# Sliding-window units behind full units 6 to 29, a cap on product runs per slot, later reciprocals

## The chip, the cores and the metric

One Trainium2 chip, one core of it. The metric is the device time of one execution in microseconds (us). Before the change three runs gave 967.66, 967.76 and 965.90 us, median 967.66.

## What is computed

Two attention blocks that share nothing but the shape: S = 2048 positions, D = 512, H = 32 heads of 16. The first ("full") attends to every position, the second ("sliding") to the last 256. The two outputs stand side by side in the last dimension.

```python
qkv = (x @ wqkv).reshape(B, S, 3, H, 16)          # q, k, v: (B, H, S, 16)
scores = einsum("bhqd,bhkd->bhqk", q, k) * 16 ** -0.5
# second block only: keep 0 <= i - j < 256, elsewhere -1e9
o = einsum("bhqk,bhkd->bhqd", softmax(scores), v)
out = concatenate([o_A @ wo_A, o_B @ wo_B], axis=-1)
```

## The kernel before, in words

**Units and slots.** Queries come in four quarters (`p`) of 512, heads in eight groups (`g`) of four, so each block has 32 units. A full unit has 64 jobs: 16 key tiles of 128 times four heads, each a 128 x 512 block of scores with keys on the partitions. A sliding unit has 12 jobs of up to 512 columns, whose scores begin with masks that TensorE adds by an identity product (line 242 into `sps`). `slots` (a method of the kernel class) lines all jobs for ScalarE up, two to a slot: one slot is one score buffer `sps` (two of them, in PSUM) and one exponential (`exps`, L521) into `pT`. There are 866 slots. The order of units is fixed: full unit k, then those sliding units whose place is k. `B_AT, B_END` spread the 32 sliding units evenly behind full units 9 to 29.

**Part of the exponentials lies on VectorE.** `D_KTS` and `D_N` give up to six of the sixteen key tiles of a full unit to VectorE, which turns a score block into an integer whose bits are an approximate exponential (`y`, L533). GpSimd, or for some VectorE, adds two shifts to it (`z`, L548), and three weighted copies of v (`va`, `v0x`, `v1x`) combine y and both z. These jobs ride as a third score matmul in a slot, in a bank of `dps`. `D_N` holds the number of such key tiles for each of the 32 full units; they sum to 175.

**Values.** `values` (L604) multiplies exponentials with v, in runs of four matmuls, one for each head in its own column group, and accumulates in one PSUM bank `op`. The first column of v is one, so that each head's first row is the sum of its exponentials. When a unit is done, `epilogue` copies the bank (`osb`, L650), gathers the four sums (`den`, a DMA, one slot later), takes the reciprocal on VectorE (`invert`, L659), sends it to DRAM and reads it back spread over 32 rows each (`rb`, L667), and multiplies on GpSimd (`on`, L673). `LAGS` holds how many slots after the copy the reciprocal, the spread read and the multiplication may start. The result goes through DRAM into `oT`, from which the output projection reads.

**Projections in between.** Keys, values, queries and outputs are projected in pieces, woven between the slots: a task is four pieces (`pieces`), each a run of four matmuls (`quad`, L242); after slot 30 there is one PSUM bank (`ms`) for all of them. After the last piece VectorE evacuates the bank. A query task also computes a bound of its scores (`magnitude`, then `guard` with `nega`, L388) which takes the bank once more. The projected keys and queries pass through DRAM scratch rows (`dka`, `dkb`, `dq`) to reach their layout.

**What sets the order.** The whole program is written out by a loop over slots in `run`, engine by engine in that order. `plan` gives each task a slot from which it may run (`nb`), a due slot and the tasks that must be done before it (`after`). In `run`, `rate` is the largest of (pieces up to a due slot) / (slots until then), at most 4; it adds to `credit`, at most 4, and each piece costs 1. In a slot `s` the loop writes: the exponential of s, DMAs that are due, VectorE's queue (`vector`), values and pieces (`fill`), then the scores of slot s + 2, then possibly one more piece. `used` counts the runs of the slot, `room` is 3, in slots that precede masked scores 2. In a slot without any run, a dummy run on mask data (`unread`) keeps TensorE at work: into the free projection bank, or, if that is taken or was just released (`extra`), into the score buffer itself ahead of the scores. A task becomes eligible when its `after` is done; DMA landings count as done a fixed number of slots after their issue (`LANDED`).

The x tiles of the sliding block take the places of the first two x tiles of the full block, so they are loaded, by a transposing DMA (L226), only when the queries of that full quarter are projected.

Of the kernel before, what the change touches and what calls it, by code (L numbers as in the profile page):

```python
# [20 lines left out]
NG = H // GH  # L21
# [5 lines left out]
S = 2048  # L27
D = 512
NC = D // P
NPASS = S // 512  # L30
# [3 lines left out]
QRING = (2, 2)  # L34
KRING_B = 6
VRING_B = 10
B_AT, B_END = 9, 29
EARLY = (0, 30)
LANDED = dict(x=14, w=10, wo=10, oT=8)
LAGS = (5, 10, 15)  # L40
ONES_BITS = 1.0019378662109375

LOG2E = 1.4426950408889634
# [5 lines left out]
BIAS = math.log(MEAN) - 127.0 * math.log(2.0)  # L49
NEG = -30000.0  # L50
D_KTS = (1, 4, 6, 9, 11, 14)
D_N = (0, 4, *(5,) * (NG - 2), *(6,) * (NPASS * NG - NG - 2), 5, 4)
D_LEAD = 24


# [52 lines left out]
class _Kernel:  # L108
# [36 lines left out]
    def scratches(self):  # L145
        zero = self.tile([P, 512], BF16, "y0", Y_BUFS)
        one = self.tile([P, 512], BF16, "y0", Y_BUFS)
        self.nc.gpsimd.memset(zero[:].bitcast(FP32), 0.0)
        self.nc.gpsimd.memset(one[:].bitcast(FP32), ONES_BITS)
        self.rows = {name: [self.dram.tile([2 * P, n], BF16, name=f"{name}{k}")  # L150
                            for k in range(bufs)]
                     for name, n, bufs in (("dq", 512, 4), ("dka", S, 2), ("dkb", 512, 3),
                                           ("do", 512, 4))}
        for name, head in (("dka", one), ("dq", None), ("dkb", one)):
            for t in self.rows[name]:
                n = t.shape[1] // 512
                t = t[:].rearrange("(h r) (c f) -> h r c f", r=32, f=512)
                self.nc.sync.dma_start(t[:, VP:, :, :], zero[0:8 * (32 - VP), :].unsqueeze(
                    1).broadcast_to((8 * (32 - VP), n, 512)))
                if head is not None:  # L160
                    self.nc.sync.dma_start(t[:, 0, :, :], head[0:8, :].unsqueeze(
                        1).broadcast_to((8, n, 512)))
# [249 lines left out]
    def q_steps(self, i, p, pr, free):  # L412
        def finish(bank):
            qs = self.q_copy(bank, self.nc.vector.tensor_copy)
            rows = self.scratch("dq")
            rows_of.append(rows)
            self.guarded += 1
            self.after(1, lambda: self.nc.sync.dma_start(rows[:, 1:VP, :], qs[:]))
            self.nega(i, pr, p)

            def magnitude():
                mq = self.q_abs(bank, qs)
                self.guards.append((self.slot + 3, lambda: guard(mq, rows)))
            return magnitude

        def guard(mq, rows):
            bank, alone = self.q_guard(i, p, pr, mq), not self.early()
            if alone:
                self.open = bank
            else:  # L430
                self.full += 1

            def lift():
                gs = self.q_lift(bank)
                if alone:
                    self.open = None
                    self.freed = self.slot
                else:
                    self.full -= 1
                self.guarded -= 1  # L440
                self.after(1, lambda: self.nc.sync.dma_start(rows[:, 0, :], gs[:]))
                self.after(max(5, free - self.slot), load)
            self.dve.append((self.slot + 1, 0.69, lift))

        def load():
            self.nc.sync.dma_start(self.q_tile(i, p, pr)[:],
                                   rows_of[0].rearrange("(g j) r f -> (j r) g f", g=2))
        rows_of = []
        return self.pieces(lambda: self.q_ops(i, p, pr)[0], lambda: self.q_ops(i, p, pr)[1],
                           finish)  # L450

    def out_steps(self, i, p, last=False):
        steps = []
# [522 lines left out]
    def plan(self, slots, done):  # L976
# [3 lines left out]
        begin, end, vneed = {}, {}, {}  # L980
# [6 lines left out]
        tasks = []  # L987
# [20 lines left out]
        for i in range(2):  # L1008
            for p, pr in q_order:
                old = before(q_order, (p, pr), QRING[i])  # L1010
                task(("q", i, p, pr), begin[i, p, 2 * pr] - (20 if (i, p, pr) == (0, 0, 1) else 28),
                     self.q_steps(i, p, pr, old and end[i, old[0], 2 * old[1] + 1] + 3 or 0),
                     [("qb",), *(("kx", 0, pr, c) for c in range(NPASS))] if i == 0
                     else [("kx", 1, pr, p), ("w", 1, 0)],
                     old and (i, old[0], 2 * old[1] + 1), 12)
            for p in range(NPASS):
                e = end[i, p, NG - 1] + LAGS[2] + 20
                if (i, p) != self.order[-1][:2]:
                    steps = self.out_steps(i, p)
                    for n in range(4):  # L1020
                        task(("o", i, p, n), e - 8 + 4 * n, steps[n * NC:(n + 1) * NC],
                             [("oT", i, p), ("wo", i)])
                    self.woven.add((i, p))
        for n, after in ((1, [("k", 0, pr) for pr in range(NPAIR)]),
# [3 lines left out]
        for c in range(NPASS):  # L1028
# [8 lines left out]
            for t in range(4 * c, 4 * c + 4):  # L1037
                old = t - VRING_B
# [3 lines left out]
            for pr in range(NPAIR):  # L1042
                old = before(q_order, (c, pr), KRING_B)
# [38 lines left out]
    def run(self):  # L1082
        self.orow, self.done, self.woven = {}, set(), set()
        self.start()
        done = self.done
        done |= {("v", 0, t) for t in range(2)} | {("q", 0, 0, 0), ("wo", 0)}
        slots = self.slots()
        tasks = self.plan(slots, done)
        credit = 0.0
        for s in range(2):  # L1090
            self.pick(s, slots[s])
            self.scores(slots[s])
        self.values_first()
        for s, sl in enumerate(slots):
            self.slot = s
            self.exps(s, sl)
            due = [x for x in self.later if x[0] <= s]
            self.later = [x for x in self.later if x[0] > s]
            for _, f in due:
                f()  # L1100
            self.vector(s, sl)
            rate, total = 0.0, 0
            for t in tasks:
                if t["nb"] <= s:
                    total += len(t["steps"])
                    rate = max(rate, total / max(1, t["due"] - s))
            credit = min(credit + min(rate, 4.0), 4.0)
            ahead = slots[s + 2] if s + 2 < len(slots) else None
            masked = bool(ahead) and bool(ahead["jobs"][0].blocks)
            room = 2 if masked else 3  # L1110
            used = self.values(s, room - (credit >= 1.0))
            while credit >= 1.0 and used < room + 1 and self.fill(s, tasks, done, False):
                credit -= 1.0
                used += 1
            if used < room:
                used += self.values(s, room - used)
            extra = False
            if len(self.banks) < 3 and self.near is not None and s >= len(slots) - 8 + 2 * len(
                    self.banks):
                tag, bufs = ("dps", 2) if len(self.banks) < 2 else ("ms", 1)  # L1120
                self.banks.append(self.ps.tile([P, 512], FP32, name=tag, tag=tag, bufs=bufs)[:])
                self.most(len(self.banks) - 1)
            elif not used and not self.banks and not self.early():
                extra = self.open is not None or s < self.freed + 2
                if not extra:
                    self.unread(self.bank()[:])
            if ahead:
                self.pick(s + 2, ahead)
                self.scores(ahead, extra)
            if (self.guards or credit >= 1.0) and (  # L1130
                    not masked or used < room or credit >= 3.0):
                if self.fill(s, tasks, done, True):
                    credit -= 1.0
                    used += 1
                while self.early() and credit >= 1.0 and used < room + 1 and self.fill(
                        s, tasks, done, True):
                    credit -= 1.0
                    used += 1
        assert not tasks, [t["name"] for t in tasks]
        while self.unit < len(self.order) or self.dve or self.later:  # L1140
            self.slot += 1
            due = [x for x in self.later if x[0] <= self.slot]
            self.later = [x for x in self.later if x[0] > self.slot]
            for _, f in due:
                f()
            self.bucket = 9.0
            self.vector(self.slot, slots[-1])
            self.values(self.slot, 1)
# [57 lines left out]
```

## Time and profile before

| engine | busy us | what for the most part |
|---|---|---|
| PE (TensorE) | 862.0 | scores, masks, values, projections |
| ACT (ScalarE) | 897.0 | 866 exponentials, L521 |
| DVE (VectorE) | 724.9 | y (L533, 700 times), evacuations, part of z |
| POOL (GpSimd) | 672.5 | z (L548, 524 half tiles), `on` (L673, 63 times) |

The profiled execution spans 966.7 us. A group in the page is read as: line, engine, operation, tile written <- tiles read, shapes, count, then busy time, mean ns of one, idle time of the engine just before, and who ended most of it. In a timeline a row is start, duration, engine, line, operation and tiles, with the idle time before and its releaser in brackets. In the answer by windows the columns are the window, its length, busy time and instruction count of PE, PEld (weight loads), DVE, ACT and POOL, the granted TensorE clock as a share of full speed, the DMA share and GB/s. In the waits a row is the waiting engine and tile, who released it, total us, times, and the longest.

DMA work is light on average: 70.02 MB in all, and the SyncE queue's packets took 23.7% of sixteen engines' span.

### The profile page before, as it was taken

To read this page: it belongs to the slowest core of one execution; us is meant where nothing else is said; L and a number is where in the kernel's file an instruction comes from. 1 tells how busy PE (TensorE), PEld (TensorE's weight loads), DVE (VectorE), ACT (ScalarE), POOL (GpSimd) and SP (SyncE) were. 2 spreads that over 40 slices of the span, in tenths; PEclk is the share of its full clock that TensorE was granted. 3 is DMA by queue.
4 is the path that set the end of the run, shared out by engine and by line. 5 is a ranking of instruction groups with operands and counts; after the bars stand their busy time and mean duration, and the time that the engine had idled before them with its cause. 6 is when DMAs were issued, how large, how long until landed. Compare 5 with 4: busy or idle time off the path is not lost.

```text
span 966.7 us, 29831 instructions
## 1 busy us (share of the span) xinstructions
PE 862.0 (89%) x12386; PEld 325.6 (34%) x12390; DVE 724.9 (75%) x1195; ACT 897.0 (93%) x883; POOL 672.5 (70%) x694
## 2 busy tenths in 40 slices
PE   7988888888899999989898889988989899898887
PEld 3322222223243324333343333433333334333322
DVE  4587987988886858878778688686886877857742
ACT  4889999999989979999999999999999999999995
POOL 2016887888858875968858678687686874976860
PEclk8999998999999979999999999999999999999978
DMA  8032314111212252122221224122212222221111
GB/s 253 14 92 92 96 41 129 57 37 40 69 57 78 83 103 62 46 81 84 64 63 63 76 71 109 57 70 81 76 56 57 85 75 64 80 74 42 41 35 44
DMA packets 84039, 70.02 MB, mean 72 GB/s; under 512 B 31080, under 2 KB 75072, under 8 KB 83904
## 3 DMA queue, kind: packets, MB, share of 16 engines
q1 hardware_dynamic: 82560, 67.60, 23.7%
q8 instruction: 96, 1.57, 0.7%
q10 hardware_dynamic: 1344, 0.52, 0.2%
q14 instruction: 39, 0.32, 0.1%
HBM read 42.73 MB, written 22.76 MB: 68 GB/s over the span
## 4 chain that ended last, share of the span: by engine, by line
ACT 46%; PE 36%; issue 11%; DVE 3%; DMA 3%; POOL 1%; SPq 0%; ACTq 0%; DVEq 0%; POOLq 0%
ACT pT L521 46%; PE sps L501 10%; PE op L604 9%; PE ms L242 7%; PE sps L242 5%; PE dps L501 2%; PE dps L242 2%; DMA da<-amax 1%; DVE y L533 1%; DMA y<-in_A_wqkv_dram 1%; PE ms L388 1%; DMA den<-osb 0%; POOL z L548 0%; PE dps L247 0%; PE dps L802 0%
## 5 line engine op out<-in xcount | busy, mean ns | idle before, releaser
L521 ACT ACTIVATE pT<-sps,bias 128x1024 bf16<-128x1024 f32 (+2 forms) x866 | 886.1, 1115 | 47.8 <-PE dps L501 24.7
L548 POOL TENSOR_SCALAR z<-y 128x1024 int16<-128x1024 int16 x524 | 570.0, 1088 | 231.4 <-DVE y L533 140.3
L533 DVE TENSOR_SCALAR y<-dps 128x512 int16<-128x512 f32 x700 | 468.0, 683 | 126.6 <-PE dps L501 111.3
L501 PE MATMUL sps<-qTa,kTa 32*128 32x512 bf16 x1348 | 265.5, 390 | 38.0 <-ACT pT L521 31.3
L501 PE MATMUL dps<-qTa,kTa 32*128 32x512 bf16 x700 | 271.8, 388 | 3.6 <-DVE y L533 1.7
L501 PEld LDWEIGHTS <-kTa 32*128 32x128 bf16 x2048 | 100.0, 91 | 255.0 <-issue 249.9
L242 PE MATMUL sps<-mask,ident 128*32 128x256 bf16 (+2 forms) x3116 | 128.0, 262 | 47.0 <-ACT pT L521 45.2
L604 PE MATMUL op<-pT,va 128*32 128x512 bf16 x1348 | 139.2, 395 | 1.1 <-ACT pT L521 0.9
L242 PEld LDWEIGHTS <-ident 128*32 128x32 bf16 x3360 | 88.8, 95 | 118.4 <-issue 101.3
L673 POOL TENSOR_TENSOR on<-osb,rb 128x512 bf16<-128x512 f32 x63 | 83.4, 1323 | 25.3 <-DMA rb<-dn 20.5
L548 DVE TENSOR_SCALAR z<-y 128x2048 int16<-128x2048 int16 x88 | 80.3, 913 | 5.2 <-PE op L604 1.0
L604 PEld LDWEIGHTS <-va 128*32 128x32 bf16 x2048 | 49.8, 95 | 82.2 <-issue 75.4
L501 PE MATMUL sps<-qTb,kTb 32*128 32x384 bf16 (+2 forms) x704 | 72.4, 276 | 0.0
L604 PE MATMUL op<-z,v1x 128*32 128x512 bf16 x700 | 71.9, 391 | 0.0
L604 PE MATMUL op<-z,v0x 128*32 128x512 bf16 x700 | 70.6, 390 | 0.0
L604 PE MATMUL op<-y,va 128*32 128x512 bf16 x700 | 69.5, 391 | 0.0
L650 DVE COPY osb<-op 128x512 f32<-128x512 f32 x63 | 42.8, 679 | 0.1
L394 DVE TENSOR_SCALAR ob<-ms 8x512 bf16<-8x512 f32 x31 | 20.9, 675 | 23.4 <-PE ms L388 22.0
L604 PE MATMUL op<-pT,vb 128*32 128x384 bf16 (+2 forms) x704 | 38.1, 280 | 0.0
L457 DVE CAST ob<-ms 128x512 bf16<-128x512 f32 x28 | 19.2, 685 | 21.5 <-PE ms L242 21.5
L242 PE MATMUL ms<-xlo,wq 128*32 128x512 bf16 x368 | 31.8, 383 | 0.5 <-DVE ob L394 0.2
L501 PEld LDWEIGHTS <-kTb 32*128 32x128 bf16 x704 | 21.0, 92 | 31.2 <-issue 27.8
(132 smaller groups left out, 491.4 us busy)
## 6 DMA issues: line engine op xcount, KB each, us to landing
rb<-dn SPq DMA_DIRECT2D x63, 256.0 KB
do<-on SPq DMA_DIRECT2D x62, 128.0 KB
kTb<-dkb SPq DMA_DIRECT2D x16, 256.0 KB
qTb<-dq SPq DMA_DIRECT2D x16, 256.0 KB
dq<-qs SPq DMA_DIRECT2D x31, 128.0 KB
qTa<-dq SPq DMA_DIRECT2D x15, 256.0 KB
out_dram<-ob SPq DMA_DIRECT2D x29, 128.0 KB
kTa<-dka SPq DMA_DIRECT2D x3, 1024.0 KB
```

What stands on the lines that cost most here:

```text
L242: self.nc.tensor.matmul(out[m], lhsT=lhsT[:, m], rhs=rhs, tile_position=(0, 32 * j), skip_group_check=True, **kw)
L388: self.nc.tensor.matmul(b[0:32, :], lhsT=self.nega(i, pr, p)[:], rhs=mq[:], start=True, stop=True, tile_position=(0, 0), skip_group_check= ...
L394: self.nc.vector.tensor_scalar(out=gs[:], in0=b[0:8, :], scalar1=LIFT, scalar2=None, op0=ALU.add)
L457: self.nc.vector.tensor_copy(out=ob[:], in_=bank)
L501: nc.tensor.matmul(at[b][:, o:o + q1 - q0], lhsT=kT[r, gg, k0:k0 + P], rhs=qT[r, gg, q0:q1], start=not jb.blocks, stop=True, tile_position ...
L521: nc.scalar.activation(out=pT[:, b:e, :n], in_=src, func=ACT.Exp, scale=SCALE, bias=self.bias[:])
L533: nc.vector.tensor_scalar(out=y[:, jb.j, :].bitcast(I16), in0=at[b], scalar1=0.0, scalar2=BITS, op0=ALU.max, op1=ALU.mult)
L548: eng.tensor_scalar(out=z[:, j:j + step].bitcast(I16), in0=grp["y"][:, j:j + step].bitcast(I16), scalar1=SHIFTS[n], scalar2=1.0, op0=ALU.a ...
L604: self.nc.tensor.matmul(u["t"][32 * j:32 * j + 32, q0:q1], lhsT=v[:, h * VP:h * VP + 32], rhs=src, start=(j not in u["started"]), stop=Fal ...
L650: nc.vector.tensor_copy(out=osb[:], in_=op[:])
L673: nc.gpsimd.tensor_mul(out=on[:], in0=osb[:], in1=st["rb"][:])
```

## The change

It moves the sliding units to full units 6 to 29, gives full unit 7 a sixth key tile on VectorE (the sum of `D_N` becomes 176), projects the second quarter of the full block's queries sooner (earlier due slots, a longer lead, eight `dq` scratch buffers instead of four, since their rows wait longer in DRAM for their place), makes the reciprocal and what follows it two slots later, gives output projections later due slots, and limits a slot to `room` runs, with one more where a task is late or the scores ahead are masked. The dummy run into the score buffer is left out ahead of masked scores. `nega` is computed with the first piece of a query task instead of after its last. The purpose is to even out TensorE's work between the slots, and to keep waits for DMAs and for GpSimd away from the queues that feed ScalarE.

```diff
-B_AT, B_END = 9, 29
+B_AT, B_END = 6, 29
-LAGS = (5, 10, 15)
+LAGS = (7, 12, 17)
-D_N = (0, 4, *(5,) * (NG - 2), *(6,) * (NPASS * NG - NG - 2), 5, 4)
+D_N = (0, 4, *(5,) * 5, *(6,) * 23, 5, 4)
...
-                     for name, n, bufs in (("dq", 512, 4), ("dka", S, 2), ("dkb", 512, 3),
+                     for name, n, bufs in (("dq", 512, 8), ("dka", S, 2), ("dkb", 512, 3),
...
-            self.nega(i, pr, p)
...
+        steps = self.pieces(lambda: self.q_ops(i, p, pr)[0], lambda: self.q_ops(i, p, pr)[1],
+                            finish)
+
+        def first(step=steps[0]):
+            self.nega(i, pr, p)
+            step()
+        return [first, *steps[1:]]
...
-                task(("q", i, p, pr), begin[i, p, 2 * pr] - (20 if (i, p, pr) == (0, 0, 1) else 28),
+                due = begin[i, p, 2 * pr] - (20 if (i, p, pr) == (0, 0, 1) else 28)
+                if (i, p) == (0, 1):
+                    due = min(due, begin[1, 1, 0] - 90 + 6 * pr)
+                task(("q", i, p, pr), due,
...
-                     old and (i, old[0], 2 * old[1] + 1), 12)
+                     old and (i, old[0], 2 * old[1] + 1), 84 if (i, p) == (0, 1) else 12)
...
-                        task(("o", i, p, n), e - 8 + 4 * n, steps[n * NC:(n + 1) * NC],
+                        task(("o", i, p, n), min(e + 6, len(slots) - 20) + 4 * n, steps[n * NC:(n + 1) * NC],
...
-            rate, total = 0.0, 0
+            rate, total, late = 0.0, 0, False
             for t in tasks:
                 if t["nb"] <= s:
+                    late = late or t["due"] < s + 2
...
-            while credit >= 1.0 and used < room + 1 and self.fill(s, tasks, done, False):
+            while credit >= 1.0 and used < room + (late or masked) and self.fill(
+                    s, tasks, done, False):
...
-                extra = self.open is not None or s < self.freed + 2
-                if not extra:
+                extra = not masked and (self.open is not None or s < self.freed + 2)
+                if self.open is None and s > self.freed + 1:
                     self.unread(self.bank()[:])
...
             if (self.guards or credit >= 1.0) and (
-                    not masked or used < room or credit >= 3.0):
+                    late or used < room or credit >= 3.0):
```

Here `e` is the last slot of the unit's quarter, plus `LAGS[2]`, plus 20.

More of the change, by code (lines that the diff above doesn't have):

```diff
@@ L448, in q_steps @@
         rows_of = []
-        return self.pieces(lambda: self.q_ops(i, p, pr)[0], lambda: self.q_ops(i, p, pr)[1],
-                           finish)
+        steps = self.pieces(lambda: self.q_ops(i, p, pr)[0], lambda: self.q_ops(i, p, pr)[1],
[4 more added lines that the diff above has]
+        return [first, *steps[1:]]
     def out_steps(self, i, p, last=False):
```

## The prediction, made before the changed kernel was run

> **What bounds the kernel now.** I read the page's busy shares first, then the costliest groups, the waits, and the timeline of single slots.
>
> From the page, busy time and groups:
>
> ```profile
> PE 862.0 (89%) x12386; PEld 325.6 (34%) x12390; DVE 724.9 (75%) x1195; ACT 897.0 (93%) x883; POOL 672.5 (70%) x694
> PEclk8999998999999979999999999999999999999978
> ...
> L521 ACT ACTIVATE pT<-sps,bias 128x1024 bf16<-128x1024 f32 (+2 forms) x866 | 886.1, 1115 | 47.8 <-PE dps L501 24.7
> L548 POOL TENSOR_SCALAR z<-y 128x1024 int16<-128x1024 int16 x524 | 570.0, 1088 | 231.4 <-DVE y L533 140.3
> L533 DVE TENSOR_SCALAR y<-dps 128x512 int16<-128x512 f32 x700 | 468.0, 683 | 126.6 <-PE dps L501 111.3
> ```
>
> ScalarE is the fullest engine, with one exponential per slot (x866). Its 93% hides something: the activations overlap at their ends. Where nothing holds it up, consecutive starts lie 1.00 us apart although one lasts 1.13 us. Numbering the starts as slots 0 to 865, the first is at 21.3 us, the last at 953.4 us. So 865 x 1.00 = 865 us is ScalarE's own pace, 67.1 us is slots longer than 1.00, and 21.3 + 13.3 us are the two ends: together 966.7. Only the 67.1 us, the number of slots and the ends can move.
>
> The timeline at 510 us shows how a slot gets too long:
>
> ```profile
> 510.69 0.39 PE L501 MATMUL sps<-qTa,kTa 32*128 32x512 bf16 x2
> ...
> 511.78 0.39 PE L501 MATMUL sps<-qTa,kTa 32*128 32x512 bf16 x2
> ...
> 512.10 0.40 PE L242 MATMUL ms<-wo,oTa 128*32 128x512 bf16 x4
> ...
> 512.33 0.39 PE L604 MATMUL op<-y,va 128*32 128x512 bf16 x4
> 512.54 0.82 PE L242 MATMUL ms<-wo,oTa 128*32 128x512 bf16 x12
> ...
> 513.29 0.39 PE L501 MATMUL sps<-qTa,kTa 32*128 32x512 bf16 x2
> ...
> 513.79 4.13 ACT L521 ACTIVATE pT<-sps,bias 128x1024 bf16<-128x1024 f32 x4 [0.40 <-PE dps L501]
> ```
>
> Three value runs of four matmuls stand between the first two score groups, which lie 1.09 us apart. Five runs, four of them pieces of an output projection, make the next interval 1.51 us, and ScalarE idles 0.40. A run costs about 0.21 us on top of some 0.43. Three runs are thus just over ScalarE's pace; four give about 1.3. Counting runs this way between score groups, and taking the starts of line 521, gives (slots from 30 on, outside the low-clock stretches below):
>
> - full slots: 0 to 2 runs, 414 slots, 3.8 us over 1.00 in total; 3 runs, 137 slots, 8.6; 4 runs, 49 slots, 9.1; 5 runs, 12 slots, 5.5
> - sliding slots (masks come first): 192 slots, 21.9 us over, of which 44 slots with an extra dummy run (`unread`) ahead of the masks in the score buffer hold 7.7
>
> Of all these, the 66 slots with two or more projection pieces hold 24.4 us; 30 of them, with 11.8 us, lie where output projections run. Slots 0 to 29 hold 6.4 us and the low-clock stretches 11.8; 48.8 + 6.4 + 11.8 = 67.0.
>
> From the waits, and the windows and timeline around the largest such stretch:
>
> ```profile
> PE sps L242 <- ACT pT L521: 45.2, 115, 0.6
> PE sps L501 <- ACT pT L521: 31.3, 108, 0.6
> ACT pT L521 <- PE dps L501: 24.7, 71, 1.4
> ...
> DVE den L659 <- DMA den<-osb: 2.2, 1, 2.2
> ```
>
> ```profile
> 349.50:360.00 10.50, 10.50 (x76) 2.15 (x72) 3.64 (x6) 6.58 (x6) 8.91 (x9) 0.51 0.19 65
> ```
>
> ```profile
> 347.59 0.25 DVE L659 RECIPROCAL den<-den 128x16 f32<-128x16 f32 x1 [2.20 <-DMA den<-osb]
> 347.76 0.63 DVE L533 TENSOR_SCALAR y<-dps 128x512 int16<-128x512 f32 x1
> 348.44 0.37 PE L501 MATMUL dps<-qTa,kTa 32*128 32x512 bf16 x1 [1.13 <-DVE y L533]
> ```
>
> PE and ScalarE wait for each other in turn, in short waits: neither is full, the sharing out is uneven. Once, VectorE reaches a reciprocal whose gather was issued at 342.97, just behind the transposing loads of a sliding x tile (338.2 and 341.1), and waits 2.20 us. The y evacuation behind it waits, PE loses 1.13 us, and for some ten microseconds the granted clock is 0.51. Slots 307 to 315 are 5.5 us over. Other such stretches: 155 to 162 (2.7), 879 (1.4), 923 (2.2).
>
> **What the skill says.** "TensorE: Matmul & The Clock Gate", Part 1: PE's clock falls to half after an idle window of about 3.4 us. The stretches agree on the half (0.51), though PE was not wholly idle before them. The same page ("Architectural detail") calls ACT and DVE strict FIFO; the trace agrees, y stood behind the reciprocal. "TensorEngine Tiling (Array Packing)", Key Properties: changing the tiling mode drains the array. That fits: a first run after scores takes 0.33 us in the chain, later ones 0.22. So many short visits are no free substitute for one long one, but a run joined to value runs costs only its 0.22.
>
> **The change, part by part.**
>
> *One more key tile on VectorE (D_N sums to 176, was 175).* Four jobs leave ScalarE, so 864 slots: -2 x 1.00 = -2.0 us. Added: 4 y at 0.683 on DVE and two shifts (about 4.4 us) on POOL, which are 75% and 70% busy, and two runs (0.43 us) on PE; hidden beside 864 activations.
>
> *Reciprocals two slots later (LAGS 7, 12, 17).* Two slots are about 2.0 us, so the one wait of 2.20 shrinks to 0.2, and the 0.51 stretch it opens should go: -5 of the 5.5 (bounds 0 and -6).
>
> *No extra run ahead of the masks.* Sliding slots without any product run average 1.144 with the extra run (39 slots) and 1.045 without (13 slots, dummy in the free bank only): 39 x 0.10 = 3.9; five slots with one run besides average 1.41 against 1.04: 1.9. I take -5 (bounds -2 and -7.7).
>
> *At most three runs, and later output projections.* Before, an output projection is due 27 slots after its last unit, while its oT is ready some 33 slots after (1 + 15 + 3 + 5 + 8 of load allowance, plus one). So it is late by construction, the rate saturates, and everything else runs in bursts with it. Now it is ready after about 35 and due after 43 to 55: 16 pieces in 20 slots, 0.8 a slot. I take three quarters of those 11.8 us away (-9) and half of the other 12.6 (-6), since `late` still allows four runs. The displaced pieces come back in other slots: 49 + 2 x 12 = 73 runs, mostly making a two-run slot a three-run one at 1.063 - 1.016 = 0.047 each: +3. Net -12 (bounds -3 and -20).
>
> *Sliding units from full unit 6.* By the slot counts the first starts at slot 166 instead of 228, so its weights and x are due at slot 106, ahead of the last keys (111) they must wait for. Tasks are flagged late there, and four runs a slot return. The 24 pieces for its first keys, queries and values, at three a burst slot, make 8 bursts of about 0.35: +3 (bounds 0 and +6). The second quarter of queries moves early because the second x tile overwrites its input; its pieces are the same number: 0. The extra `dq` buffers add four zero fills at the start; the four there take 2.69 us of the queue at 16 to 19 us, and the queue then waits 26.3 us for amax from 23.9: hidden.
>
> *nega at the first piece.* PE and its weight load wait for it 1.0 + 1.2 us in total: -1.
>
> *The end.* The last oT arrives two slots later in a run two slots shorter, so 16 pieces have 12 slots, not 14; slots 850 to 865 are 1.8 over now: +1.
>
> Added waits: none by design. Should the first sliding loads land late, PE's scores wait, and behind them everything queued on PE, then ScalarE.
>
> Sum: -2 - 5 - 5 - 12 + 3 - 1 + 1 = -21, so 967.7 - 21 = 946.7 us.
>
> **Rivals.**
> 1. *The bursts only move* (chance 0.18). With one free bank, a task holds it for its pieces plus evacuation; slowed, tasks fall behind, `late` is set often, and four runs return. For: PE is 89% busy. Against: outside bursts most slots have no more than two runs. Then -2 - 5 - 3 + 3 = -7: 960.
> 2. *Slower* (0.12). The earlier sliding loads meet the last kTa load (1 MB) and the early stores, and new waits of the 347 us kind appear, each a 2 to 3 us wait plus a half-clock stretch, 8 us in all. Four of these eat 32 us against -21: 978. For: transposing loads caused one. Against: three of the four x loads caused none, and reciprocals get two slots of slack.
> 3. *Almost all of it goes* (0.18). Bursts -20, dummies -7, the wait -6, slots -2, no early crunch: -35, 932.
> 4. *It cancels* (0.04): 967.
>
> **Numbers.** The main case has 0.48 and lies between 939 and 955. Faster: 0.48 + 0.18 + 0.18 = 0.84, of which I give 0.02 away for parts that interact; same 0.05; slower 0.13. The range leaves out the best of rival 3 and most of rival 2: 926 to 968.
>
> **What would show it.** 864 activations and no reciprocal waiting over 1 us; no granted clock near 0.5 around an x load; few stretches of five runs, and output projections spread over 20 slots; sliding slots nearer 1.03. The sum over 1.00 should fall from 67 to some 47 us. It would be wrong if waits for sliding keys or queries appeared near slot 166 (some 195 us), or if ScalarE's waits on PE stayed at 40 us or more.

## The result, and the profile after

The changed kernel takes 956.08 us (median of six runs, 951.68 to 961.85), the one before 967.32: ratio 0.9893, 95% interval 0.9854 to 0.9933. It is faster, by 11 us where 21 were forecast. Its runs lie ten us apart, those of before beside it two; the profiled run, at 961.31, is one of the slower ones, which matters below.

From the page, the lines that answer to those of before. The exponential is now line 525, the shifts 552, the y evacuation 537:

```profile
PE 859.3 (90%) x12074; PEld 317.0 (33%) x12074; DVE 733.4 (76%) x1199; ACT 892.1 (93%) x881; POOL 676.1 (70%) x698
PEclk9999999999989999999999999999999999999967
...
L525 ACT ACTIVATE pT<-sps,bias 128x1024 bf16<-128x1024 f32 (+1 forms) x864 | 881.3, 1114 | 45.5 <-PE dps L505 26.3
L552 POOL TENSOR_SCALAR z<-y 128x1024 int16<-128x1024 int16 x528 | 575.8, 1091 | 235.3 <-DVE y L537 110.1
L537 DVE TENSOR_SCALAR y<-dps 128x512 int16<-128x512 f32 x704 | 470.6, 683 | 99.0 <-PE dps L505 88.7
```

864 exponentials, and 312 matmuls fewer in the trace: 81 dummy runs of four are left out, and a few come with the new key tile. ScalarE still idles 45.5 us ahead of them, so what was gained is not to be seen in that row. It is to be seen in the slots. With the starts of line 525 read as before, the profiled run is 62.2 us over a pace of 1.00 us, where before it was 67.1:

| slots, us over 1.00 each | before | after |
|---|---|---|
| full, 0 to 2 runs | 414 slots, 3.8 | 405, 1.8 |
| full, 3 runs | 137, 8.6 | 164, 10.5 |
| full, 4 runs | 49, 9.1 | 18, 4.3 |
| full, 5 runs | 12, 5.5 | 4, 1.8 |
| sliding | 192, 21.9 | 192, 13.7 |
| sum, outside low-clock stretches | 48.8 | 32.0 |
| low-clock stretches from slot 30 on | 11.8 | 22.6 |
| slots 0 to 29 | 6.4 | 7.6 |

The part the change aims at shrank by 16.8 us. The low-clock stretches took 10.8 of it back in this run.

The runs in this table, as in the prediction's count, are the program's `used` and not quite what stands between two score groups, as the prediction says: a piece that is written after the scores counts in its own slot, but in the trace it stands ahead of the next score group. Counted in the trace between score groups, four or more runs stand in 67 intervals before (20.8 us over pace) and in 53 after (12.4 us), three runs in 131 and 132. The excess shrinks by as much as in the table; but the long intervals become fewer by a fifth only, where `used` says by two thirds (61 to 22).

The timeline of TensorE inside an output projection, which answers to the five runs at 512 us of before:

```profile
574.54 0.43 PE L505 MATMUL sps<-qTa,kTa 32*128 32x512 bf16 x2
...
575.88 0.39 PE L505 MATMUL sps<-qTa,kTa 32*128 32x512 bf16 x2
...
576.20 0.62 PE L608 MATMUL op<-y,va 128*32 128x512 bf16 x8
576.64 0.39 PE L242 MATMUL ms<-wo,oTb 128*32 128x512 bf16 x4
576.97 0.39 PE L505 MATMUL sps<-qTa,kTa 32*128 32x512 bf16 x2
...
577.29 0.40 PE L608 MATMUL op<-pT,va 128*32 128x512 bf16 x4
577.51 0.39 PE L242 MATMUL ms<-wo,oTb 128*32 128x512 bf16 x4
577.84 0.39 PE L505 MATMUL sps<-qTa,kTa 32*128 32x512 bf16 x2
```

From 575.88 on one piece of the projection stands in an interval, beside one or two value runs: 1.09 and 0.87 us from score group to score group, where before one took 1.51. It is not so everywhere: the interval from 574.54 holds two pieces and two value runs and took 1.34 us, and one like it, from 578.62, took 1.30.

The waits:

```profile
PE sps L242 <- ACT pT L525: 36.5, 96, 0.6
PE sps L505 <- ACT pT L525: 32.2, 115, 1.2
ACT pT L525 <- PE dps L505: 26.3, 43, 3.9
DVE den L663 <- DMA den<-osb: 5.7, 3, 5.0
```

TensorE's waits ahead of masks fell from 45.2 us to 36.5. ScalarE waits for TensorE's `dps` scores 43 times instead of 71, but the longest is 3.9 us instead of 1.4, and VectorE's waits for the gather of `den` rose from 2.2 to 5.7 us, against the purpose of the later reciprocals. The timeline shows the longest:

```profile
864.52 0.52 POOL L711 MEMSET wk<- 128x512 f32 x1
...
865.08 1.75 SPq L713 DMA_DIRECT2D wk<-in_A_wo_dram  x4
...
867.42 0.59 SPq L659 DMA_DIRECT2D den<-osb  x1
...
869.60 0.25 DVE L663 RECIPROCAL den<-den 128x16 f32<-128x16 f32 x1 [4.96 <-DMA den<-osb]
...
870.45 0.37 PE L505 MATMUL dps<-qTa,kTa 32*128 32x512 bf16 x1 [3.59 <-DVE y L537]
...
872.16 2.21 ACT L525 ACTIVATE pT<-sps,bias 128x1024 bf16<-128x1024 f32 x2 [3.89 <-PE dps L505]
```

The padded output weights (`pad_wo`) need a memset, which stands in GpSimd's queue until 864.52. Their loads wait for it at the head of SyncE's queue, the gather behind them leaves at 867.42, the reciprocal waits 4.96 us on VectorE, the y behind it, TensorE 3.59, ScalarE 3.89. It is the same chain as at 347 us before, with another transfer at its head.

The low-clock stretches, by windows. Each pair is the 3.4 us ahead of a stretch and its first 3.4 us (busy time and instructions of PE, PEld, DVE, ACT, POOL; granted clock, DMA share, GB/s). First the changed kernel:

```profile
567.80:571.20 3.40, 2.42 (x32) 0.97 (x29) 3.27 (x6) 3.40 (x4) 0.00 (x0) 1.00 0.32 106
571.20:574.60 3.40, 3.40 (x33) 0.76 (x30) 2.29 (x5) 2.75 (x3) 1.70 (x2) 0.51 0.27 71
711.20:714.60 3.40, 2.32 (x29) 0.93 (x29) 3.37 (x7) 3.40 (x5) 1.94 (x2) 1.00 0.29 82
714.60:718.00 3.40, 3.34 (x30) 0.86 (x30) 0.86 (x3) 2.71 (x4) 1.06 (x2) 0.50 0.05 7
...
600.00:603.40 3.40, 3.40 (x52) 1.03 (x54) 2.52 (x4) 3.40 (x5) 1.76 (x2) 1.00 0.12 25
```

and the kernel before, ahead of its stretch at 879:

```profile
875.40:878.80 3.40, 2.19 (x33) 0.92 (x26) 2.94 (x6) 3.23 (x5) 0.94 (x1) 1.00 0.24 81
878.80:882.20 3.40, 3.39 (x30) 0.81 (x29) 2.31 (x4) 2.70 (x3) 0.18 (x1) 0.50 0.06 10
```

TensorE does not stand still ahead of these stretches: ScalarE runs at full pace in the changed kernel's two windows (3.40 of 3.40) and TensorE is busy two thirds of the window, with 29 to 33 matmuls. Then the clock is halved just when three-run slots follow. In an ordinary window (600 us) TensorE is busy throughout.

These windows are examples. In each of the 14 profiles of this case all changes to half clock lie on one grid of 3.41 us. Taking the windows of this grid between 30 and 945 us that ran at full clock, and asking after which the clock was halved:

| TensorE busy in the window, us of 3.41 | windows | half clock followed |
|---|---|---|
| under 2.4 | 78 | 52 |
| 2.4 to 2.5 | 58 | 14 |
| 2.5 to 2.7 | 221 | 23 |
| 2.7 to 3.0 | 768 | 5 |
| over 3.0 | 2445 | 0 |

So light windows are what the half clock follows, but the busy time as the profile models it is no sharp limit: in the changed kernel a window with 2.06 us (864.8) was passed over and one with 2.88 (356.2) was not.

### The profile page after: what moved, and what is told of

Read it like the earlier page. It is cut to its first block, busy times and chain, and to the rows that moved or that the text cites. A ratio compares the mean times of both kernels' runs of the same rounds, so it can differ in the third digit from the quotient of the medians.

```text
span 959.6 us, 29202 instructions
## 1 busy us (share of the span) xinstructions
PE 859.3 (90%) x12074; PEld 317.0 (33%) x12074; DVE 733.4 (76%) x1199; ACT 892.1 (93%) x881; POOL 676.1 (70%) x698
## 5 line engine op out<-in xcount | busy, mean ns | idle before, releaser
L525 ACT ACTIVATE pT<-sps,bias 128x1024 bf16<-128x1024 f32 (+1 forms) x864 | 881.3, 1114 | 45.5 <-PE dps L505 26.3
L552 POOL TENSOR_SCALAR z<-y 128x1024 int16<-128x1024 int16 x528 | 575.8, 1091 | 235.3 <-DVE y L537 110.1
L505 PE MATMUL dps<-qTa,kTa 32*128 32x512 bf16 x704 | 275.2, 391 | 7.9 <-DVE y L537 5.3
L505 PEld LDWEIGHTS <-kTa 32*128 32x128 bf16 x2048 | 102.9, 91 | 262.8 <-issue 257.2
L242 PE MATMUL sps<-mask,ident 128*32 128x256 bf16 (+2 forms) x2824 | 111.6, 256 | 37.7 <-ACT pT L525 36.5
L242 PEld LDWEIGHTS <-ident 128*32 128x32 bf16 x3036 | 77.7, 95 | 100.6 <-issue 85.4
L552 DVE TENSOR_SCALAR z<-y 128x2048 int16<-128x2048 int16 x88 | 84.7, 963 | 7.3 <-PE op L608 5.4
L608 PE MATMUL op<-z,v1x 128*32 128x512 bf16 x704 | 74.5, 398 | 0.0
L394 DVE TENSOR_SCALAR ob<-ms 8x512 bf16<-8x512 f32 x31 | 20.8, 671 | 23.4 <-PE ms L388 20.9
L377 DVE CAST qs<-ms 128x512 bf16<-128x512 f32 x31 | 21.1, 682 | 16.5 <-PE ms L242 16.4
```

Of the source, the lines that this page charges most:

```text
L242: self.nc.tensor.matmul(out[m], lhsT=lhsT[:, m], rhs=rhs, tile_position=(0, 32 * j), skip_group_check=True, **kw)
L377: copy(out=qs[:], in_=bank)
L394: self.nc.vector.tensor_scalar(out=gs[:], in0=b[0:8, :], scalar1=LIFT, scalar2=None, op0=ALU.add)
L505: nc.tensor.matmul(at[b][:, o:o + q1 - q0], lhsT=kT[r, gg, k0:k0 + P], rhs=qT[r, gg, q0:q1], start=not jb.blocks, stop=True, tile_position ...
L525: nc.scalar.activation(out=pT[:, b:e, :n], in_=src, func=ACT.Exp, scale=SCALE, bias=self.bias[:])
L552: eng.tensor_scalar(out=z[:, j:j + step].bitcast(I16), in0=grp["y"][:, j:j + step].bitcast(I16), scalar1=SHIFTS[n], scalar2=1.0, op0=ALU.a ...
```

## What was tested

The theory after this: the change evens out the runs as meant, but it also leaves out dummy runs (119 are left of 200), which would make light stretches lighter, and the half clock takes part of the gain back; the wait at 869 us adds to it. Rivals: the stretches only follow VectorE's waits for DMAs; or TensorE is the limit and the displaced runs themselves cost what is missing.

For every kernel the runs give span and mean granted clock. (1 - clock) x span is the clock time lost in a run; span minus that is a rough measure of what the program would take without it (rough, since over the runs of one kernel a lost us cost between 0.5 and 1.0 us where the number varied enough to tell). Means over each kernel's runs; the ratios are to the kernel before on the same chip:

| kernel | dummy runs | ratio (95% interval) | clock | lost, us | span less lost, us |
|---|---|---|---|---|---|
| before (43 runs beside e5 to e8) | 200 | 1 | 0.977 | 22.5 | 944.5 |
| the change | 119 | 0.9893 (0.9854 to 0.9933) | 0.972 | 26.6 | 928.4 |
| e1 more dummies | 334 | 0.9819 (0.9787 to 0.9851) | 0.987 | 12.1 | 939.8 |
| e2 no dummy | 0 | 0.9924 (0.9891 to 0.9958) | 0.953 | 44.9 | 917.3 |
| e3 padded weights later | 119 | 0.9799 (0.9758 to 0.9839) | 0.976 | 22.5 | 927.4 |
| e4 dummy ahead of masks back | 155 | 0.9911 (0.9877 to 0.9946) | 0.970 | 28.5 | 932.3 |
| e5 both e1 and e3 | 334 | 0.9776 (0.9742 to 0.9811) | 0.993 | 6.9 | 937.4 |
| e6 outputs due early | 117 | 0.9907 (0.9874 to 0.9940) | 0.973 | 26.2 | 931.0 |
| e7 cap undone | 119 | 1.0011 (0.9990 to 1.0031) | 0.963 | 35.9 | 932.3 |
| e8 lags undone | 109 | 0.9925 (0.9901 to 0.9948) | 0.967 | 32.1 | 927.3 |
| e9 sliding place undone | 136 | 0.9909 (0.9874 to 0.9944) | 0.972 | 27.0 | 931.3 |
| e10 cap alone, on the kernel before | 190 | 1.0023 (1.0002 to 1.0044) | 0.972 | 27.2 | 943.2 |
| e11 dummy after light slots | 228 | 0.9765 (0.9735 to 0.9795) | 0.987 | 12.3 | 932.0 |
| e12 fewer of these | 178 | 0.9773 (0.9740 to 0.9806) | 0.985 | 14.1 | 932.3 |

The runs were on different chips. Beside e1 to e4 the kernel before lost 24.7 us, beside e9 to e12 23.8; and single runs of the change lost between 21 and 34. A difference of two or three us of lost time between two rows is therefore within what chips and chance do.

### More dummies, and none (e1, e2)

```diff
-            elif not used and not self.banks and not self.early():
+            elif used <= (0 if masked else 1) and not self.banks and not self.early():   # e1
+            elif False:                                                                  # e2
```

> The changed kernel, with the dummy run on mask data written also into full slots that have one real run, not only into those that have none. Theory (half clock): the changed kernel writes 119 dummy runs where the one before wrote 200, so more windows of light TensorE work end in half-clock stretches, 22.6 us over pace against 11.8; with the dummies the granted clock should rise from 0.968 to 0.98 or more, the stretches between 30 and 940 us fall from nine to three or fewer, and the time to about 947 us with less spread between runs. Rival (waits): the stretches follow VectorE's waits for a DMA (at 62 and 869 us), so at most 3 us is gained. Rival (displaced runs): TensorE is the limit, an added 0.16 to 0.2 us of work makes it slower, about 960 us.

> The changed kernel without any dummy run after slot 30. Theory (half clock): the granted clock falls to 0.95 or less, many more half-clock stretches, 970 us or more. Rival (waits): within 3 us of the changed kernel's 956. Rival (displaced runs): less TensorE work, so 952 to 956 us.

With 215 more dummies the clock rises to 0.987 and the nine stretches between 30 and 940 us shrink to two, at 37 us (before dummies are written at all) and at the wait of 866 us. Without dummies it falls to 0.953, and the page shows stretches all over:

```profile
PEclk9999999899999999997999999999999999997978
```

The lost clock time goes 44.9, 26.6, 12.1 us with 0, 119 and 334 dummies: that the dummies hold the clock is shown. It fits the order of the program: with dummies counted as runs, three neighbouring slots, none of them ahead of masks, hold at most three runs together 84 times in e2, 50 times in the change and twice in e1. Both sizes were less than expected, because dummies cost work (by the ratios, on the basis of 967.3 us, 950 us instead of 947, and 960 instead of 970 or more): 917.3, 928.4 and 939.8 us without the lost time, some 0.05 to 0.09 us each. In e1 the three-run slots are 14.7 us over instead of 10.5. So the rival of TensorE as the limit seems to hold for part: a dummy takes slack that heavy slots would use. Whether e2 differs from the change at all is open; the intervals overlap.

### The wait behind the padded weights (e3), and both (e5)

```diff
-        for j in range(GH):
-            self.nc.sync.dma_start(self.wop[32 * j + 1:32 * j + 1 + DH, :, :], ...)
+        def rows():
+            for j in range(GH):
+                self.nc.sync.dma_start(self.wop[32 * j + 1:32 * j + 1 + DH, :, :], ...)
+        self.after(12, rows)
```

> The changed kernel, with the four small loads of the padded last output weights issued 12 slots after the memset that they wait for, so that the SyncE queue does not stand behind GpSimd's queue at 862 to 865 us. The 4.96 us wait of the reciprocal at 869.6 us, the 3.9 us idle of ScalarE and the half-clock stretch after it should be gone. Theory (half clock): 4 to 5 us gained, 951 to 952 us, the other stretches stay. Rival (waits): other waits of that kind are small, so no more than that either; if the wait only moves to another load in the queue, nothing is gained, 956 us.

> The changed kernel with both single changes that helped: the dummy run also in full slots with one real run, and the four padded-weight loads 12 slots later. If the two causes are separate (half-clock stretches; SyncE's queue behind GpSimd), the gains add: the first alone stood at a ratio of 0.982 to the kernel before, the second at 0.980, the changed kernel at 0.989, so about 0.973, with a granted clock of 0.985 or more and no reciprocal waiting over 2 us. If it is one cause (the wait drags the clock down), it stays near 0.980.

In e3 the loads leave after the gathers, at 863.19 us, and no reciprocal waits over 1.3 us:

```profile
859.66 0.58 SPq L659 DMA_DIRECT2D den<-osb  x1
...
863.19 2.40 SPq L715 DMA_DIRECT2D wk<-in_A_wo_dram  x4
```

```profile
DVE den L663 <- DMA den<-osb: 1.8, 3, 1.3
```

The ratio is 0.0094 below the change's, some 9 us, and the intervals do not overlap. The medians themselves, from two chips, differ by 4.5 us (951.5 and 956.1), which is what was expected, and the table has 4.1 us less lost clock and 1.0 us less of the rest. So 4 to 5 us are accounted for; what the ratio has over that may be chance or the chip.

Both together reach 946.04 us. The clock is at full almost throughout, TensorE busy 93%:

```profile
PE 878.5 (93%) x12934; PEld 320.5 (34%) x12934; DVE 731.5 (78%) x1199; ACT 892.6 (95%) x881; POOL 677.2 (72%) x698
...
PEclk9999999999999999999999999999999999999998
```

0.9776 lies between the two answers expected and does not tell them apart by itself. The profile does: with both, no stretch is left between the start (slot 2) and the last exponential, with e1 alone the one behind the wait was. The profiled run is 46.8 us over pace. That this is the number forecast for the change itself (47) is a coincidence: e5 carries 215 dummies more, which cost work.

### The dummy ahead of the masks (e4)

```diff
-                extra = not masked and (self.open is not None or s < self.freed + 2)
+                extra = self.open is not None or s < self.freed + 2
```

> The changed kernel with the extra dummy run ahead of the masks put back. By the step of the prediction, 5 us slower in sliding slots (the changed kernel's sliding slots are 8.2 us less over pace than before). Theory (half clock): some of it is given back by a higher granted clock, net 956 to 960 us. Rival (displaced runs): the dummy did not matter, 956 us.

The sliding slots are 18.5 us over pace instead of 13.7: 4.8 us, where the prediction took 5. In the table the span less lost rises by 3.9 us. The clock did not rise (0.970). 0.9911 against 0.9893 is within the intervals. So this dummy costs about what was said and buys no clock that can be seen. It also speaks against these 36 of the 81 dummies left out as a reason for the change's lower clock.

### Due slots, cap, lags, places (e6 to e9)

```diff
-                        task(("o", i, p, n), min(e + 6, len(slots) - 20) + 4 * n, ...)
+                        task(("o", i, p, n), e - 8 + 4 * n, ...)                        # e6
-            while credit >= 1.0 and used < room + (late or masked) and self.fill(
+            while credit >= 1.0 and used < room + 1 and self.fill(                      # e7
-                    late or used < room or credit >= 3.0):
+                    not masked or used < room or credit >= 3.0):                        # e7
-LAGS = (7, 12, 17)
+LAGS = (5, 10, 15)                                                                      # e8
-B_AT, B_END = 6, 29
+B_AT, B_END = 9, 29                                       # e9, with D_N and the q due slots
```

> The changed kernel with the output projections due as before (14 slots sooner), so that they are late by construction again. Prediction's step: 9 of the 12 us come from here, so about 6 to 9 us slower, ratio 0.995 to 0.998, with over 30 slots of two or more pieces in the stretches of output projections. Rival (the cap alone limits the bursts): no change, 0.989.

> The changed kernel with the old limits on runs in a slot (four in a full slot, the last piece of a masked slot only below two runs). If the cap itself removes bursts, four- and five-run slots come back and it is 4 to 6 us slower, 0.993 to 0.995. Rival (later due slots alone did it, rates are low enough): no change, 0.989.

> The changed kernel with the old lags (5, 10, 15). Prediction's step: two slots of slack are worth one wait and its half-clock stretch, 5 us, so 0.993 to 0.995, and one or more further reciprocals wait for their gather, over 2 us. Rival: with the sliding units at other places the gathers no longer meet the transposing loads, only the wait behind the padded weights counts and grows by 2 us, 0.991.

> The changed kernel with the sliding units behind full units 9 to 29 again, the old D_N (one key tile less on VectorE, 866 slots) and the old due slots and lead of the second quarter of queries. Prediction's steps: the two slots cost 2 us and the early crunch of 3 us goes, so 1 us faster than the changed kernel, ratio 0.988. Rival (fewer sliding units per full unit and an earlier second x tile even out the work): 4 us or more slower, 0.993 or above.

*e6.* 1.4 us slower by the ratios, within the intervals, not the 6 to 9 expected. Slots with two or more pieces, at least one of an output projection, go from 20 to 28, their excess from 6.6 to 10.1 us. So the due slots do what was said of them, at less than half the size.

*e7.* The whole gain is gone: 1.0011 against 0.9893, far outside both intervals, and twice the 4 to 6 us expected. In the profile four- and five-run slots come back (`used` goes from 22 to 54 slots outside the stretches; in the trace 53 intervals become 56, with 17.4 us over pace instead of 12.4), and the span less lost rises by 3.9 us. But the lost clock time is larger still, 35.9 us against 26.6. The windows ahead of its stretches are light ones again, and half clock lasts longer in one piece:

```profile
237.20:240.60 3.40, 2.31 (x53) 0.97 (x49) 3.40 (x5) 1.86 (x4) 3.24 (x3) 1.00 0.26 80
240.60:247.40 6.80, 6.41 (x51) 1.61 (x50) 5.43 (x9) 4.86 (x5) 3.74 (x5) 0.50 0.32 97
```

So undoing the cap costs some 4 us of longer bursts and about 9 us of lost clock time. One would say that the same pieces done in bursts leave more light slots between them, but the order of the program hardly shows it: three neighbouring slots with at most three runs occur 54 times here, 50 times in the change and 50 times in the kernel before. The profile has seven stretches between 30 and 940 us, where the change has nine; they are longer, 58 us in all instead of 48. How the cap comes to hold the clock is open.

*e8.* 0.9925 against 0.9893: the lags may be worth 3 us; the intervals overlap. One reciprocal waits 5.6 us, the one behind the padded weights, and no other one, as the rival said, though it is 0.7 us longer than in the change and not two. With the old lags, then, the wait of before at 347 us does not come back.

*e9.* 0.9909, 1.6 us slower and within the intervals. The forecast crunch is hard to find: slots 100 to 199 are 2.4 us over in the changed kernel and 2.1 here (4.2 in the kernel before, 2.7 of them in its stretch at 155 us). Something else changed with the places. In e9 no gather stands behind the loads of the padded weights (they leave at 841.22), and no reciprocal at all waits for its gather. The wait of 5 us thus came with the places or what was changed for them, not with the lags: e8 has it with the old lags, e9 is without it with the new ones. A fairer comparison for the places is e3, which has them without the wait: 0.9799 against 0.9909, intervals apart, so they and what goes with them (the key tile, the due slots) may be worth some 10 us once the wait is out of the way.

### The cap alone (e10)

```diff
-            while credit >= 1.0 and used < room + 1 and self.fill(s, tasks, done, False):
+            while credit >= 1.0 and used < room + (late or masked) and self.fill(
+                    s, tasks, done, False):
...
-                    not masked or used < room or credit >= 3.0):
+                    late or used < room or credit >= 3.0):
```

> The kernel before with the cap alone: `late`, room + (late or masked), and the condition of the last piece; output projections stay late by construction, so `late` holds through them. If the cap is the main part by itself, 0.988 to 0.992. If it works only where little is late, because of the later due slots and the spread of the sliding units, no gain: 0.998 to 1.002.

No gain, 1.0023. Without the cap the rest of the change brings nothing (e7), and the cap without the rest brings nothing either. By `used`, four- and five-run slots go from 61 to 38 here and three-run slots from 137 to 179; between score groups in the trace the intervals of four runs and more only go from 67 to 65 (20.8 to 16.0 us over pace), since the cap does not count the piece that the slot before wrote after its scores. The lost clock time did not fall, it is 27.2 us against 23.8 on the same chip: the cap by itself does not hold the clock. The profile has stretches with long slots (4.6 us at 708 us). Undoing the due slots alone (e6) loses little, so they are not the partner that the cap needs. The places may be: e9 loses little, but it loses the wait with them. Which of the rest the cap needs is open.

### Where a dummy pays (e11, e12)

```diff
-            elif not used and not self.banks and not self.early():
+            elif (not used or (used == 1 and not masked and sum(hist[-2:]) <= 3)) \
+                    and not self.banks and not self.early():     # e11; e12 has <= 2
...
+            hist.append(used)      # runs of each slot; and the padded weights as in e3
```

> The changed kernel with the padded-weight loads later, and the dummy run in a full slot with one real run only where that slot and the two before it hold at most four runs: 228 dummy runs, between the changed kernel's 119 and the 334 of the version with all. If dummies cost in proportion (11 us for 215 of them with no low clock counted) and the half clock comes only from light windows, it keeps most of the clock at half the cost: granted clock 0.985 or more, ratio about 0.973. If every dummy buys clock in proportion to its cost, between the two, 0.978.

> As the one before with at most three runs in the three slots: 178 dummy runs. Same two answers: granted clock 0.98 and ratio 0.974 if only the light windows count, about 0.979 if clock and cost trade evenly.

Against e3, which shares the later loads, 59 more dummies placed where three slots together hold at most three runs (e12) take 8.4 us off the lost clock time and cost 4.9 us of work; 109 (e11) take off 10.2 for 4.6, and 215 in all light slots (e5) 15.6 for 10.0. The first ones thus buy most, which speaks for the light windows: three neighbouring slots with at most three runs occur 7 times in e12 and 6 times in e11, against 50 in e3. Yet the times, 946.2 and 946.4 us, do not differ from e5's 946.0: 0.9765, 0.9773 and 0.9776. The three are the fastest kernels here, 2.2 to 2.4% below the kernel before and 1.2 to 1.3% below the change, with intervals that lie outside the change's. In e11 and e12 the clock and the cost of work balance against e5 within what the runs can tell, so neither of the two expected answers is singled out.

## Why the prediction was right, and where it was off

The direction, and the mechanism of long slots, were right; the size was about half of what was forecast. Step by step:

- *Two slots fewer, -2.* 864 exponentials, as said; their time was not measured apart.
- *Extra dummy, -5.* Right: sliding slots 8.2 us less over pace, and 4.8 of them come back in e4; the other 3.4 were not traced to a part of the change.
- *Cap and later outputs, net -12.* Right in kind, too large: the full slots' excess fell by 8.6 us in the profile; three-run slots grew by 1.9 where 3 were added. That e7 loses 11 us, close to the 12, is luck: some 9 us of lost clock time, which the step did not name, and 3.9 us of the rest. The 9 us put down to the later due slots are 1.4 by the times of e6 and 3.5 by its slots. The cap is needed for the gain (e7), but does not make it alone (e10).
- *Lags, -5.* This step failed. The wait at 347 us went, and its stretch with it, but nothing shows that the lags did it: it is absent with the old lags too (e8, and e10 with the old places). And a wait of 4.96 us came at 869, with the places (e9). The prediction named the transposing x loads as what delays a gather. What it left out is that a transfer ahead of the gather in SyncE's queue can itself wait, here for GpSimd. In total 5.7 us of such waits instead of 2.2.
- *Earlier sliding units, +3.* Hardly seen: outside low-clock stretches slots 100 to 199 are 2.4 us over instead of 1.5. The step left out what the places would do elsewhere, the wait at 869 us against it and perhaps 10 us for it (e9 against e3).
- *nega, -1.* Its waits are 1.4 us now (one wait of the weight load, behind GpSimd's z), 2.2 before: right in sign, of no weight.
- *The end, +1.* Slots from 850 on are 5.1 us over instead of 1.8, most of the difference in a low-clock stretch at 930 us.
- *Left out: the clock.* The forecast kept the other stretches as they were and priced the dummies at their work alone. This is the term that was missing. Stretches hold 22.6 us in the profiled run instead of 11.8, but that run is one of the slower ones; over all runs the lost clock time is 26.6 us, where the kernel before lost 22.5 to 24.7, with 16 us saved otherwise (944.5 to 928.4). The prediction quoted the Trainium skill's account of the clock ("TensorE: Matmul & The Clock Gate", Part 1, half clock after an idle window), and saw that TensorE was not wholly idle ahead of these stretches, but drew nothing from it. The windows above say that here two thirds busy is often little enough.

In this rough division the miss lies in the clock. The steps without the lags add up to -16, and the span less lost fell by 16, partly by luck, since it is made of steps that came out larger and smaller and of a new wait. The -5 of the lags stood for a low-clock stretch of 10 us that was to go, that is, for 5 us of lost clock time; the lost time did not fall but rose by 2 to 4. That it did not fall by 5 is outside the scatter of the runs (the lowest lost 21 us, where 5 less than before is 17 to 20); that it rose is not. Why the change's clock is no better than before is not settled: fewer dummies were the theory, but the 36 ahead of masks make none that can be seen (e4), and the light groups of three slots are as many as before (50).

The sum over pace was to fall from 67 to 47 us; it fell to 62 in the profiled run. Two of the signs that were named came out against the forecast there: a reciprocal waited over 1 us (4.96), and ScalarE's waits for TensorE ahead of the exponentials stayed at 40.4 us (42.6 before), where 40 or more was to show it wrong. Rival 1 (960 us) named late tasks as the danger; what came instead was the clock.

## What to carry to other kernels

Where dummy work holds TensorE's clock, leaving some out or moving real work has two prices, the work and the lost clock: read granted clock times span for every run, not the profiled one alone. A cap on bursts must count what stands between two score groups, or it lets long intervals through; and undo each part of a change, for here the cap alone gained nothing and its removal cost the whole gain. A lag of two slots ahead of a consumer did not protect it against a transfer that stood in its issuing queue behind one that waited for another engine.

## What was not expected of the hardware

- The clock was halved after windows of 3.4 us in which TensorE was busy 2.2 to 2.4 us; no idle window was needed. The changes lie on a grid of 3.41 us, and of 2445 windows in which TensorE was busy over 3.0 us none was followed by half clock.
- The same program's runs then lie apart: the change's six runs had granted clocks of 0.965 to 0.978 and times of 961.9 to 951.7 us, in that order. On the three chips of e1 to e12 the kernel before ran from 962 to 976 us.
- Over the runs of one kernel a us of lost clock cost 0.7 us in the kernel before, 0.85 in the changed one. The profile of the changed kernel says why it is not more: wholly within half-clock stretches, most full slots with one run between their score groups still took 1.05 to 1.09 us, those with three 1.6 to 1.95.
